# Third expert's rows gathered during the first expert's second product, and row traffic spread alike for all experts

## The chip, the cores and the metric

The kernel runs on one core of a Trainium2 chip. The metric is the time of one execution in device microseconds (us). Five engines work side by side, each with its own instruction queue in program order: PE (TensorE, matrix products), DVE (VectorE), ACT (ScalarE), POOL (GpSimd) and SP (SyncE, which here only issues transfers). Transfers (DMA) are issued by SP or POOL and then run on 16 DMA engines by themselves.

## The reference

Three stages follow one another: a decaying linear attention, a mixture of eight experts of which each row uses two, and a SoLU block. The middle stage is the one that the change touches:

```python
logits = x @ w_gate
noisy_logits = logits + np.log1p(np.exp(x @ w_noise)) * noise
top2 = np.argpartition(-noisy_logits, 2, axis=1)[:, :2]      # two experts for each of 1536 rows
...
for e in range(E):                                           # E = 8, D = 512, F = 1024
    for k in range(2):
        mask = top2[:, k] == e
        h = np.maximum(x[mask] @ w1[e], 0.0)                 # first product
        out[mask] += top2_w[mask, k, None] * (h @ w2[e])     # second product
```

All in float32.

## The kernel before

The experts are taken in an order by their number of rows, the first with room for 448 rows and the last for 384. The text calls them e0 to e7 in that order, so "the third expert" is e2. For each expert the program has a **first product** (`hidden`, L693: eight groups f = 0 to 7 of 12 matmuls, four by `xh` with two weights each and four by `xl`) and a **second product** (`second`, L1030: four steps j = 0 to 3 of 24 matmuls). A float32 product is made of three matmuls on a high and a low part: `split_unit` makes `wh` (ACT, L194) and `wl` (DVE, L195) from each raw weight tile `wr`; `xg_t` makes `xh` (ACT, L995) and `xl` (DVE, L996) from the rows of the next expert, in four pieces d = 0 to 3, during the second product of the expert before it.

How the rows of an expert reach `xg_t` is what the change is about. `load_xg(e)` is a generator whose steps are called from the main loop:

- up to four gathers on POOL (L959), each of 128 rows of `xd` (DRAM) into a buffer `xr` (on-chip);
- the stores of `xr` to `xs` in DRAM on SP (L969), two a step;
- the loads of `xq` from `xs` on SP (L976), two a step. These put the rows into 32x32 blocks, so that `xg_t` can turn them with a DVE transpose (`xt`, L993).

For e1 there is only the gather: PE transposes those rows itself (L989). For e2 and later all three steps are needed. In the kernel before, e2 gathers in the steps f = 0 to 3 of e1's first product, stores in f = 4 and 5 and loads in f = 6 and 7, while e3 gathers in f = 4 to 7 of the same product and stores and loads in j = 0 to 3 of e1's second product. All later experts do as e3 does, one expert earlier than they are needed. A one-element copy `pace` on POOL (L1060, L1068) ahead of a gather makes POOL wait for the result of group f. All experts share four `xr` buffers.

The order on each engine is the order in which the program issues. Around the change, SP's queue also has the weight loads (L176, `load_unit`; a load waits until the tile that it overwrites has been split), the stores of the finished rows (`yg`, L1017, in f = 5), and a conversion of the last block's weights that runs in pieces in between (`convert`: load `raw` L102, store `co` L125, work on DVE L117 to L124). `advance` splits the next weight units and issues loads for up to three units beyond. `weights()` (DVE, L661 to L679) runs once, in e1's second product.

Of the kernel before, what the change touches and what calls it, by code (L numbers as in the profile page):

```python
# [8 lines left out]
F32 = mybir.dt.float32  # L9
# [35 lines left out]
def retnet_moe_solu(ctx, tc, qT, kT, k, v, w_gate, w_noise, noise, w1, w2, w_in, w_out, g_ln,  # L45
                    decay, out, dbg=None):
    nc = tc.nc
# [4 lines left out]
    E = w1.shape[0]  # L52
    DM = H * D
# [39 lines left out]
    def convert_steps():  # L93
        V = nc.vector
        cv = conv_ctx.enter_context(tc.tile_pool(name="cv", bufs=1, side="right", reuse_waits="tile"))
        view = lambda x, c: x.rearrange("(p r) f -> p (r f)", p=128)[:, c:c + 512]

        def load(n):
            if n < len(conv_jobs):
                w, _, c = conv_jobs[n]  # L100
                t = cv.tile([128, 512], I64, tag="raw", name="raw", bufs=2)
                nc.sync.dma_start(t, view(w, c))  # L102
                raws.append(t)

        raws = []
        load(0)
        for n, (w, f, c) in enumerate(conv_jobs):
            load(n + 1)
            yield
            raw = raws.pop(0)  # L110
            bits = raw.bitcast(I32).rearrange("p (n t) -> p n t", t=2)
            l, h = raw.bitcast(U32).rearrange("p (n t) -> p n t", t=2)[:, :, 0], bits[:, :, 1]
            m, e = (cv.tile([128, 512], I32, tag=t, name=t) for t in ("cm", "ce"))
            t = cv.tile([128, 512], F32, tag="ct", name="ct")
            o = cv.tile([128, 512], F32, tag="co", name="co", bufs=2)

            V.tensor_scalar(m, h, 0xFFFFF, 1 << 20, op0=OP.bitwise_and, op1=OP.bitwise_or)  # L117
            V.scalar_tensor_tensor(t, l, 2.0 ** -32, m, op0=OP.mult, op1=OP.add)
            V.tensor_scalar(e, h, 0x7FF00000, None, op0=OP.bitwise_and)
            nc.scalar.activation(e, e, AF.Relu, bias=rebias, scale=8.0)  # L120
            yield

            V.scalar_tensor_tensor(e, h, -2 ** 31, e, op0=OP.bitwise_and, op1=OP.bitwise_or)
            V.scalar_tensor_tensor(o, t, 2.0 ** -20, e.bitcast(F32), op0=OP.mult, op1=OP.mult)  # L124
            nc.sync.dma_start(view(f, c), o)  # L125

    conv = convert_steps()

    def convert():
        next(conv, None)  # L130
# [87 lines left out]
    px = ex_ctx.enter_context(tc.tile_pool(name="px", bufs=1))  # L218
# [170 lines left out]
    for b in range(B):  # L389
        for r in range(2):  # L390
            t = wk.tile([128, HP, 128], F32, name=f"S{b}{r}", bufs=1)
# [180 lines left out]
    def add_table(lo):  # L572
        oh, nm = HOT.pop(lo)
        last = oh.shape[1] - 1
        p = bank("a", (128, 32))
        for n in range(last + 1):
            nc.tensor.matmul(p, oh[:, n], nm[:, n], start=(n == 0), stop=(n == last))
        nc.vector.tensor_add(table, table, p)  # L578
# [3 lines left out]
    def by_rows():  # L582

        m = [128, 4, 32]
        nc.vector.tensor_mul(spread, part4[:, :, None].to_broadcast(m), table[:, None, :].to_broadcast(m))
# [27 lines left out]
    def first_xt(part, d):  # L613

        n = BLKS[2 * part][1]
        p = bank("a", (128, 2, 2 * n)) if n <= 128 else None
        for s in range(2):
            for b in range(2):
                nc.tensor.transpose(p[:, s, b * n:(b + 1) * n], x0[2 * part + b][:n, (d + s) * 128:(d + s + 1) * 128],
                                    ident[:n, :n])  # L620
        hi, lo = xgT[0]
        at = BLKS[2 * part][0]
        nc.scalar.activation(hi[:, d:d + 2, at:at + 2 * n], p, AF.Copy)
        nc.vector.tensor_sub(lo[:, d:d + 2, at:at + 2 * n], p, hi[:, d:d + 2, at:at + 2 * n])
# [24 lines left out]
    pace = const.tile([1, 1], F32, name="pace")  # L649

    def lists():

        p = bank("a", (128, E - 1, 4))
        nc.tensor.matmul(p, spread.rearrange("p a i -> p (a i)"), sort.rearrange("p e s -> p (e s)"),
                         start=True, stop=True)
        nc.vector.tensor_scalar_min(rows_r, p, float(NT * 128 - 1))
# [27 lines left out]
    def hidden(e, f, c):  # L684

        xh, xl = xgT[e]
        hh, hl = H_t[e]
        early_part = not e and c.start == 0
        p = bank(("b", "c0", "b", "c1")[f % 4] if early_part else "ba"[f % 2])[:, :c.stop - c.start]

        terms = [(unit_t[8 * e + d][n], x, d) for x, ns in ((xh, (0, 1)), (xl, (0,))) for d in range(KD) for n in ns]
        for n, (w, x, d) in enumerate(terms):
            nc.tensor.matmul(p, w[:, 0, f * 128:(f + 1) * 128], x[:, d, c],  # L693
                             start=(n == 0), stop=(n == len(terms) - 1))
        nc.scalar.activation(hh[:, f, c], p, AF.Relu)  # L695
        nc.vector.scalar_tensor_tensor(hl[:, f, c], p, 0.0, hh[:, f, c], op0=OP.max, op1=OP.subtract)

    H_t = {}
# [5 lines left out]
    def hidden_of(e):  # L704
        H_t[e] = (ep.tile([128, KF, CAP], F32R, tag="hh", name="hh"),
                  ep.tile([128, KF, CAP], F32R, tag="hl", name="hl"))
# [241 lines left out]
    for p in range(2):  # L948
        first_xt(1, 2 * p)

    def load_xg(e):

        if e >= E:
            return

        n = SETS[e]
        t = [px.tile([128, DM], F32, tag="xr", name="xr", bufs=4) for b in range((n + 3) // 4)]
        for b in range(len(t)):
            nc.gpsimd.indirect_dma_start(  # L959
                out=t[b], out_offset=None, in_=xd[:],  # L960
                in_offset=bass.IndirectOffsetOnAxis(ap=rows_r[:, e - 1, b:b + 1], axis=0))
            yield
        if e == 1:
            xr_t[e] = t
            return
        xs = dram.tile([ROOM, DM], F32, tag="xs", name="xs", bufs=2)
        for b in range(len(t)):
            m = min(128, 32 * n - 128 * b)
            nc.sync.dma_start(xs[b * 128:b * 128 + m, :], t[b][:m])  # L969
            if b == 1:  # L970
                yield
        yield
        x = xr_t[e] = ep.tile([128, CAP // 32, 128], F32, tag="xq", name="xq", bufs=2)
        src = xs[:32 * n, :].rearrange("(b i) (a c) -> a i b c", i=32, a=4)
        for a in range(4):
            nc.sync.dma_start(x[32 * a:32 * a + 32, :n], src[a])  # L976
            if a == 1:
                yield
# [60 lines left out]
            convert()  # L1039
        feed(up, up + 3)  # L1040

    rows = None
    for e in range(E - 1):
        if e:
            hidden_of(e)
        for j in range(4):
            for f in (2 * j, 2 * j + 1):
                hidden(e, f, slice(0 if e else EARLY, CAPS[e]))
                if not e and f == 0:
                    add_table(4)  # L1050
                    add_table(10)
                    by_rows()
                if not e and f == 2:
                    lists()
                    for _ in load_xg(1):
                        pass
                    rt_ctx.close()
                if e == 1 and f < 4:
                    rows = rows or load_xg(2)
                    nc.gpsimd.tensor_copy(pace, H_t[e][0][:1, f, :1])  # L1060
                    next(rows)
                elif e and f > 3:
                    if e == 1:
                        next(rows, None)
                    if f == 4:
                        fresh = load_xg(e + 2)
                    if e + 2 < E:
                        nc.gpsimd.tensor_copy(pace, H_t[e][0][:1, f, :1])  # L1068
                        next(fresh)
                if f in (1, 3, 4, 5):  # L1070
                    d = (1, 3, 4, 5).index(f)
                    if e:
                        y_t(e - 1, d)
                    y_bank(e, d)
                elif e and f in (2, 6):
                    convert()
            advance(e, j)
        for j in range(4):
            unit_t.pop(8 * e + j)
        xgT.pop(e)  # L1080
        py = PY[e]
        for j in range(4):
            second(e, j, py)
            for d in ((0,), (1, 2), (3,), ())[j]:
                xg_t(e + 1, d)
            if e == 1 and j == 1:
                weights()
            advance(e, 4 + j)
            if e:
                next(fresh, None)  # L1090


    for _ in conv:
        pass
    e = E - 1
# [17 lines left out]

    w2_of = [unit_t.pop(8 * e + 4 + j) for j in range(4)]
    conv_ctx.close()
    m2_ctx = ExitStack()
    feed(n_units - 2, n_units)
    fr = m2_ctx.enter_context(tc.tile_pool(name="fr", bufs=2, side="right", reuse_waits="tile"))
# [204 lines left out]
```

## Time and profile before

| | |
|---|---|
| time, median of 3 runs | 557.49 us (556.52 to 558.67) |
| profiled execution | 557.17 us, of which the span of the trace is 555.4 us |
| PE busy | 523.2 us, 94% of the span |
| DVE, ACT, POOL busy | 367.1 us, 230.8 us, 100.8 us |
| mean granted TensorE clock | 0.959 of full speed |
| DMA | 111.92 MB, mean 202 GB/s |

The profiled execution lies 0.32 us under the median. "Busy" counts time in which an instruction runs; what matters for the end is where PE, the engine with most work, has to wait, and for whom.

### The profile page before, as it was taken

The numbers are of one execution on the slowest core, as the hardware profiler recorded it, in microseconds if no ns is written. First come the engines' busy times: TensorE is split into PE (matmuls) and PEld (weight loads), VectorE is DVE, ScalarE is ACT, GpSimd is POOL, SyncE is SP. The second block draws the span as 40 slices with busy tenths as digits, with TensorE's granted clock in tenths as the row PEclk, the third lists the DMA queues.
The fourth block names the chain that finished last, engine by engine and source line by source line (L and its number), as shares of the span: only waits on it lengthen the run. The fifth ranks groups of instructions, "written<-read, shape, count | busy, mean of one in ns | idle before, by whom it ended". The sixth has DMA issues, their size and how long they took to land.

```text
span 555.4 us, 8653 instructions
## 1 busy us (share of the span) xinstructions
PE 523.2 (94%) x3107; PEld 476.7 (86%) x3107; DVE 367.1 (66%) x718; ACT 230.8 (42%) x426; POOL 100.8 (18%) x202
## 2 busy tenths in 40 slices
PE   7999989799999279999999999999989999999996
PEld 6898968699998179999999999999868888888886
DVE  3577675657850788787787867887536677576650
ACT  2377712245520335344343433534544545444441
POOL 3000011040431004013030030000044463241110
PEclk9799987899999579999999999999999999999999
DMA  8898514256789289799799897885853456555431
GB/s 243 316 321 288 190 30 136 73 180 204 255 245 243 78 251 263 287 209 343 245 265 322 188 336 234 214 232 150 234 152 114 142 149 220 155 150 141 106 114 43
DMA packets 71857, 111.92 MB, mean 202 GB/s; under 512 B 9760, under 2 KB 37152, under 8 KB 71808
## 3 DMA queue, kind: packets, MB, share of 16 engines
q1 hardware_dynamic: 65520, 94.58, 58.1%
q0 software_dynamic: 4944, 16.39, 9.6%
q8 instruction: 26, 0.43, 0.3%
q10 hardware_dynamic: 1344, 0.34, 0.3%
q14 instruction: 23, 0.19, 0.1%
HBM read 83.50 MB, written 27.79 MB: 200 GB/s over the span
## 4 chain that ended last, share of the span: by engine, by line
PE 52%; DVE 15%; DMA 13%; issue 8%; ACT 6%; SPq 3%; POOL 2%; DVEq 0%; POOLq 0%; ACTq 0%
PE b L915 12%; PE d L828 12%; PE b L693 6%; PE c L1030 6%; PE a L693 6%; DVE wl L195 3%; DMA xq<-xs 3%; DMA wr<-in_moe_w_dram 2%; DVE xt L993 2%; DMA yg<-yr 2%; PE c L439 2%; PE c L473 2%; PE s L422 2%; DMA xr<-xd,rows_r 2%; ACT xh L995 1%
## 5 line engine op out<-in xcount | busy, mean ns | idle before, releaser
L195 DVE TENSOR_TENSOR wl<-wr,wh 128x1024 fp32r<-128x1024 f32 x68 | 81.6, 1220 | 21.6 <-ACT wh L194 20.9
L1030 PE MATMUL c<-hh,wh 128*128 128x448 f32 (+5 forms) x224 | 79.2, 354 | 0.3 <-DVE c L1004 0.3
L1030 PE MATMUL c<-hh,wl 128*128 128x448 f32 (+5 forms) x224 | 78.8, 352 | 0.0
L1030 PE MATMUL c<-hl,wh 128*128 128x448 f32 (+5 forms) x224 | 78.6, 351 | 0.0
L194 ACT ACTIVATE wh<-wr 128x1024 fp32r<-128x1024 f32 x68 | 69.8, 1050 | 9.1 <-DMA wr<-in_moe_w_dram 9.1
L693 PE MATMUL b<-xh,wh 128*128 128x192 f32 (+8 forms) x144 | 49.6, 351 | 15.2 <-ACT xh L995 14.9
L693 PE MATMUL b<-xh,wl 128*128 128x192 f32 (+8 forms) x144 | 48.2, 342 | 0.0
L693 PE MATMUL a<-xh,wh 128*128 128x256 f32 (+7 forms) x128 | 44.8, 353 | 0.6 <-DVE table L578 0.6
L693 PE MATMUL a<-xh,wl 128*128 128x256 f32 (+7 forms) x128 | 44.2, 349 | 0.0
L693 PEld LDWEIGHTS b<-xh,wh 128*128 128x128 f32 x144 | 28.4, 197 | 18.2 <-ACT xh L995 17.4
L995 ACT ACTIVATE xh<-xt 128x428 fp32r<-128x428 f32 (+5 forms) x24 | 12.9, 539 | 74.6 <-DVE xt L993 72.5
L1030 PEld LDWEIGHTS c<-hh,wh 128*128 128x128 f32 x224 | 42.1, 188 | 1.7 <-issue 0.6
L1030 PEld LDWEIGHTS c<-hl,wh 128*128 128x128 f32 x224 | 42.2, 188 | 1.1
L1030 PEld LDWEIGHTS c<-hh,wl 128*128 128x128 f32 x224 | 42.1, 188 | 1.2
L789 POOL DMA_INDIRECT y<-yg,slot_y x24 | 24.0, 1001 | 84.6 <-DMA yg<-y 73.7
L828 PE MATMUL d<-wh,x2h 128*128 128x512 f32 x96 | 38.7, 403 | 0.6 <-issue 0.6
L915 PE MATMUL b<-wh,zh 128*128 128x512 f32 (+1 forms) x104 | 38.4, 375 | 0.0
L915 PE MATMUL b<-wl,zh 128*128 128x512 f32 (+1 forms) x104 | 38.3, 375 | 0.0
L828 PE MATMUL d<-wh,x2l 128*128 128x512 f32 x96 | 37.7, 393 | 0.4 <-DVE x2l L813 0.4
L828 PE MATMUL d<-wl,x2h 128*128 128x512 f32 x96 | 37.4, 390 | 0.0
L1068 POOL COPY pace<-hh 1x1 f32<-1x1 f32 x20 | 10.7, 537 | 132.9 <-ACT hh L695 132.4
L993 DVE STREAM_TRANSPOSE xt<-xq 128x416 f32<-128x416 f32 (+2 forms) x24 | 21.9, 912 | 18.6 <-DMA xq<-xs 18.6
(235 smaller groups left out, 1092.7 us busy)
## 6 DMA issues: line engine op xcount, KB each, us to landing
wr<-in_moe_w_dram SPq DMA_DIRECT2D x60, 512.0 KB
zd<-zs SPq DMA_DIRECT2D x40, 128.0 KB
zc<-zd SPq DMA_DIRECT2D x10, 512.0 KB
xs<-xr SPq DMA_DIRECT2D x18, 256.0 KB
raw<-in_moe_w_in_dram SPq DMA_DIRECT2D x8, 512.0 KB
raw<-in_moe_w_out_dram SPq DMA_DIRECT2D x8, 512.0 KB
xq<-xs SPq DMA_DIRECT2D x16, 208.0 KB
yg<-yr SPq DMA_DIRECT2D x16, 208.0 KB
```

The lines of the kernel that those rows point to most:

```text
L194: nc.scalar.activation(hi, t, AF.Copy)
L195: low = lambda: nc.vector.tensor_sub(lo, t, hi)
L422: nc.tensor.matmul(p[:, s, hp, :], KT[i][r, hp, :], QT[i][r, hp, :], start=True, stop=True)
L439: nc.tensor.matmul(py[s * 64:s * 64 + 64, hp, :], VP[i][:, 2 * hp + s, :], PM[i][hp // 2][:, hp % 2, s, :], start=(not c), stop=True, skip ...
L473: nc.tensor.matmul(lg_all[:, i], XT[i][:, d, :], wgn[:, d, :], start=(d == 0), stop=(d == KD - 1))
L693: nc.tensor.matmul(p, w[:, 0, f * 128:(f + 1) * 128], x[:, d, c], start=(n == 0), stop=(n == len(terms) - 1))
L789: nc.gpsimd.indirect_dma_start(out=t, out_offset=None, in_=yg[:upto], in_offset=bass.IndirectOffsetOnAxis(ap=slot_y[:, i, s:s + 1], axis=0))
L828: nc.tensor.matmul(PH[i][:, s, :], x[:, c], w[:, 0, f], start=(n == 0), stop=(n == 3 * KD - 1))
L915: nc.tensor.matmul(p, z[:, f * 128:(f + 1) * 128], unit_t[8 * E + 4 + f // 2][n][:, f % 2, c], start=(m == 0), stop=(m == len(terms) - 1))
L993: nc.vector.transpose(t[:, :32 * n], xr_t[e][:, :n, d:128:KD])
L995: nc.scalar.activation(hi, t, AF.Copy)
L1030: nc.tensor.matmul(py[d][:, :CAPS[e]], c, h[:, f, :CAPS[e]], start=(f == 0 and n == 0), stop=(f == KF - 1 and n == 2))
```

## The change

A pool `gx` of four `xr` buffers is opened in e0's first product, once the routing stage's memory is free; e1's rows stay in the old buffers, those of e2 and later go to `gx`. The tile `ct` of the conversion goes away (its values overwrite `cm`), so the conversion's tiles take 2 KB less in each partition and `gx` takes 8 KB.

e2 now gathers in e0's second product (two gathers each in j = 0 and 1, without a `pace`), and stores in j = 2 and 3. For e3 and later the gathers stay in f = 4 to 7 two products ahead; the stores move from j = 0 and 1 to j = 1 and 2, and the loads from j = 2 and 3 to f = 1 and 3 of the next first product. e2's loads stand in f = 1 and 3 of e1's first product likewise.

```diff
-            t = cv.tile([128, 512], F32, tag="ct", name="ct")
+            t = m.bitcast(F32)
...
+    gx = {}
+    gx_ctx = ExitStack()
+
     def load_xg(e):
...
-        t = [px.tile([128, DM], F32, tag="xr", name="xr", bufs=4) for b in range((n + 3) // 4)]
+        t = [(px if e == 1 else gx["pool"]).tile([128, DM], F32, tag="xr", name="xr", bufs=4) for b in range((n + 3) // 4)]
...
-    rows = None
...
                     rt_ctx.close()
-                if e == 1 and f < 4:
-                    rows = rows or load_xg(2)
+                    gx["pool"] = gx_ctx.enter_context(tc.tile_pool(name="gx", bufs=1, side="right"))
+                if e and f in (1, 3):
+                    next(rows, None)
+                if e and e + 2 < E and f > 3:
+                    fresh = fresh if f > 4 else load_xg(e + 2)
                     nc.gpsimd.tensor_copy(pace, H_t[e][0][:1, f, :1])
-                    next(rows)
-                elif e and f > 3:
-                    if e == 1:
-                        next(rows, None)
-                    if f == 4:
-                        fresh = load_xg(e + 2)
-                    if e + 2 < E:
-                        nc.gpsimd.tensor_copy(pace, H_t[e][0][:1, f, :1])
-                        next(fresh)
+                    next(fresh)
...
             advance(e, 4 + j)
-            if e:
+            if not e:
+                fresh = fresh if j else load_xg(2)
+                for n in range(2 if j < 2 else 1):
+                    next(fresh)
+            elif j in (1, 2):
                 next(fresh, None)
+        rows = fresh
...
     conv_ctx.close()
+    gx_ctx.close()
```

On POOL, behind the loads of e1's first weights, the program had a `pace` ahead of each of e2's gathers. Of before:

```order
L176 DMA wr<-in_moe_w_dram 128x1024
L176 ISA
L176 DMA wr<-in_moe_w_dram 128x1024
L1060 CAST pace<-hh 1x1
L959 DMA xr<-xd,rows_r 128x512
L1060 CAST pace<-hh 1x1
L959 DMA xr<-xd,rows_r 128x512
```

Of the change, at the same place:

```order
L176 DMA wr<-in_moe_w_dram 128x1024
L176 ISA
L176 DMA wr<-in_moe_w_dram 128x1024
L962 DMA xr<-xd,rows_r 128x512 x4
L1065 CAST pace<-hh 1x1
L962 DMA xr<-xd,rows_r 128x512
```

The four gathers of e2 stand right behind the weight loads; the next `pace` is that of e3's first gather.

On SP, in e1's first product, e2's four stores stood behind e1's and e2's weight loads and ahead of e0's results, and its four loads behind these. Of before:

```order
L125 DMA w_in_70<-co 128x512
L102 DMA raw<-in_moe_w_in_dram 128x512
L176 ISA
L176 DMA wr<-in_moe_w_dram 128x1024
L969 DMA xs<-xr 128x512 x3
L969 DMA xs<-xr 64x512
L1017 DMA yg<-yr 32x14x128 x4
L176 ISA
L176 DMA wr<-in_moe_w_dram 128x2x512
L976 DMA xq<-xs 32x14x128 x4
```

Of the change, from the first weight load of e2 on:

```order
L176 DMA wr<-in_moe_w_dram 128x1024
L972 DMA xs<-xr 128x512 x3
L972 DMA xs<-xr 64x512
L979 DMA xq<-xs 32x14x128 x2
L176 ISA
L176 DMA wr<-in_moe_w_dram 128x1024
L176 ISA
L176 DMA wr<-in_moe_w_dram 128x1024
L125 DMA w_in_70<-co 128x512
L102 DMA raw<-in_moe_w_in_dram 128x512
L979 DMA xq<-xs 32x14x128 x2
```

Stores and first two loads moved ahead of two of e2's weight loads, and the last two loads ahead of e2's fourth weight load and of e0's results.

On SP, in e5's first product (the rows are those of e6, the weights too). Of before:

```order
L176 DMA wr<-in_moe_w_dram 128x1024
L976 DMA xq<-xs 32x13x128 x4
L176 ISA
L176 DMA wr<-in_moe_w_dram 128x1024
L176 ISA
L176 DMA wr<-in_moe_w_dram 128x1024
L125 DMA w_out_71<-co 128x512
L102 DMA raw<-in_moe_w_out_dram 128x512
```

Of the change:

```order
L972 DMA xs<-xr 32x512
L979 DMA xq<-xs 32x13x128 x2
L176 ISA
L176 DMA wr<-in_moe_w_dram 128x1024
L176 ISA
L176 DMA wr<-in_moe_w_dram 128x1024
L125 DMA w_out_71<-co 128x512
L102 DMA raw<-in_moe_w_out_dram 128x512
L979 DMA xq<-xs 32x13x128 x2
```

Two of the four loads moved behind two weight loads, a store of the conversion and its next load.

## Rows read from the trace of the kernel before

**Rows 1.** Busy time by stretch (us); last columns: granted clock, DMA share, GB/s.

```profile
130.00:140.00 10.00, 10.00 (x53) 9.27 (x52) 8.19 (x12) 5.21 (x8) 0.00 (x0) 1.00 0.79 250
...
178.90:203.50 24.60, 9.70 (x27) 7.22 (x27) 17.59 (x35) 7.38 (x11) 0.00 (x0) 0.58 0.52 148
...
240.00:400.00 160.00, 159.69 (x876) 157.73 (x876) 122.92 (x191) 70.56 (x105) 17.91 (x23) 1.00 0.89 249
```

**Rows 2.** Waits, whole span: us in total, times, longest.

```profile
DVE xt L993 <- DMA xq<-xs: 18.6, 1, 18.6
...
PE b L693 <- ACT xh L995: 14.9, 4, 7.3
```

**Rows 3.** Timeline of PE, end of e1's second product: start, duration, instruction.

```profile
178.72 0.36 PE L1030 MATMUL c<-hl,wh 128*128 128x448 f32 x1
178.92 0.37 PE L1030 MATMUL c<-hh,wl 128*128 128x448 f32 x1
182.13 0.73 PE L693 MATMUL b<-xh,wh 128*128 128x428 f32 x1 [2.85 <-ACT xh L995]
```

**Rows 4.** Chain of waits, 120 to 300 us: start, duration, what.

```profile
152.86 8.96 DMA xr<-xd,rows_r
...
169.88 10.45 DMA xq<-xs
180.46 0.98 DVE xt L993
...
196.82 0.57 ACT xh L995
197.43 2.51 PE b L693 x6
199.94 3.58 PE a L693 x12
203.51 2.36 PE b L693 x12
...
255.40 4.89 DMA wr<-in_moe_w_dram
```

**Rows 5.** Timeline of POOL.

```profile
122.34 0.54 POOL L176 DMA_DIRECT2D wr<-in_moe_w_dram  x1 [2.47 <-DVE wl L195]
...
146.59 1.02 POOL L959 DMA_INDIRECT xr<-xd,rows_r  x1 [0.53 <-ACT hh L695]
...
164.33 0.97 POOL L959 DMA_INDIRECT xr<-xd,rows_r  x1 [9.42 <-DMA xs<-xr]
```

**Rows 6.** Tile xr: time from issue to landing of its gathers.

```profile
DMA to landing us min/median/max: 5.6/7.9/9.0
```

**Rows 7.** Timeline of SP.

```profile
144.05 0.34 SPq L176 DMA_DIRECT2D wr<-in_moe_w_dram  x1
...
144.63 0.34 SPq L176 DMA_DIRECT2D wr<-in_moe_w_dram  x1
...
196.68 0.87 SPq L969 DMA_DIRECT2D xs<-xr  x2
...
202.77 0.85 SPq L976 DMA_DIRECT2D xq<-xs  x2
...
318.68 0.43 SPq L102 DMA_DIRECT2D raw<-in_moe_w_out_dram  x1
```

**Rows 8.** Timelines of ACT and DVE, end of e1's first product.

```profile
155.44 1.05 ACT L194 ACTIVATE wh<-wr 128x1024 fp32r<-128x1024 f32 x1
...
161.25 0.62 DVE L696 SCALAR_TENSOR_TENSOR hl<-a,hh 128x448 fp32r<-128x448 f32 x1 [1.22 <-ACT hh L695]
```

**Rows 9.** Timelines of DVE, ACT and PE, from e5's second product to e6's first.

```profile
330.16 0.91 DVE L993 STREAM_TRANSPOSE xt<-xq 128x416 f32<-128x416 f32 x1
...
342.34 0.53 ACT L995 ACTIVATE xh<-xt 128x388 fp32r<-128x388 f32 x1 [2.97 <-DVE xt L993]
...
342.92 0.45 PE L693 MATMUL b<-xh,wh 128*128 128x388 f32 x1
```

## The prediction

> **What bounds the kernel now.** I read the busy time by stretch first [rows 1]. From 240 to 400 us, nearly five experts long, PE is busy for 159.69 of 160 us at the full granted clock: there the matmuls are the bound, and no transfer is worth anything. The stretch from 178.9 to 203.5 us is different: PE is busy for 9.70 of 24.60 us, the granted clock falls to 0.58 (so much of it ran at 1.2 GHz instead of 2.4), and the DMA share is only 0.52. Next the waits [rows 2]: PE waited 14.9 us in four waits for `xh`, and DVE once 18.6 us for `xq`. PE's timeline places it [rows 3]: the last matmul of e1's second product starts at 178.92, and the first of e2's first product at 182.13. Last the chain of waits [rows 4], which says why: e2's last gather is issued at 152.86 and lands 8.96 us later, stores and loads follow, the last `xq` load has been issued by 169.88 and lands 10.45 us later, and only at 180.46 can DVE begin `xt`. The fourth piece of `xh` ends at 196.82 + 0.57 = 197.39. The cause stands on POOL [rows 5]: its last weight load ends at 122.88, and the first gather of e2 runs only at 146.59, after the result of e1's first group.
>
> **What the stall costs.** Matmuls of this kind start 178.92 - 178.72 = 0.20 us apart [rows 3], so unbroken work would have begun e2 at 179.12. A group of 12 takes 2.36 us at full clock [rows 4]; two groups would end at 183.84. They ended at 199.94 + 3.58 = 203.52 [rows 4]. So 19.7 us is the most that this place can give. In it, the last 6 and the next 12 matmuls took 2.51 + 3.58 = 6.09 us where 18 at full clock take 3.54: 2.55 us of the 19.7 is the slow clock after the wait.
>
> **The change, part by part.**
>
> *Gathers of e2.* Four `pace` copies go, and the four gathers run from 122.88, some 1.3 us apart (164.33 and its successors are of that kind [rows 5]), so to about 128. At the slowest landing of a gather, 9.0 us [rows 6], all are there by 137. I cost them nothing: PE works on e0's second product, and the DMA share in 130 to 140 is 0.79 [rows 1], so there is some room for 1 MB. Without that room they would hold e1's later weights back by 1 MB at 250 GB/s [rows 1], 4 us.
>
> *Stores and loads of e2.* On SP the stores stand behind e2's first weight load, which was issued at 144.05 [rows 7]; that does not move, so they start at 144.4. Two stores take 0.87 us [rows 7], four end at 146.2. The first two loads must wait until the stores have landed: for e3 that was from 196.68 + 0.87 = 197.55 to 202.77, 5.2 us [rows 7]. So SP stands until 151.4: **this is a new wait**, with two of e2's weight loads behind it. The two loads take 0.85 us [rows 7], the two weight loads some 0.9, the conversion's store and load 0.9, and the second two loads end at about 155.1. For their landing I have 5.6 us, the fastest gather [rows 6], to 10.45 us, `xq` itself beside e3's gathers [rows 4]: 160.7 to 165.5. These gathers no longer wait 9.4 us for `xs` [rows 5] and start near 155, so the same company remains, and I take 8 us: 163.1.
>
> The Trainium skill's page "DMA: Bandwidth & Descriptors", section "Anatomy of one DMA — SWDGE (gpsimd) path", fits a transfer alone at about 2.0 us plus its bytes over 436 GB/s. By it the two loads (448 KB) would take an estimated 3.1 us and land at 158.2; no wait of DVE for them would be left, and the sum below would come out at an estimated 538.3 us. By the row of 10.45 us, three times as long for these transfers in company, it would be 539.8; the measurement decides which is nearer.
>
> *What waits behind SP.* The second of e2's weight loads was issued at 144.63 [rows 7] and would now go out near 152.7. A weight load landed 4.89 us after its issue elsewhere [rows 4]: 157.6. ACT split that tile at 155.44 [rows 8], so ACT and then DVE come 2.2 us later. DVE's last work for e1's first product ended at 161.25 + 0.62 = 161.87 [rows 8]; now about 164.0. From there DVE turns e2's rows. In the old trace that took from 180.46 to 197.39, 16.9 us (four transposes and splits, three weight splits, `weights()`, a conversion), with all data there, and I see nothing that shortens it. So `xh` is complete at 164.0 + 16.9 = 180.9. PE needs the fourth piece at the seventh matmul of e2, 179.12 + 6 x 0.20 = 180.3. Residue: 0.6 us. At the lower ends it is nothing (161.87 + 16.9 = 178.8, 1.5 us early), at the upper 165.5 + 16.9 - 180.3 = 2.1 us, with the slow clock 4.7. I take 1.0.
>
> *Stores and loads of e3 to e7.* Moving the stores by one step costs nothing while PE has 16 to 18 us of second product to cover them. The loads lose more. Closest is e6: in the new order its last two loads follow the conversion's load, issued at 318.68 [rows 7], and end near 320.1. DVE wants them at 330.16 [rows 9]: 10.0 us for landing. The fourth `xh` of e6 ends at 342.34 + 0.53 = 342.87 and PE takes it at 342.92 [rows 9], so there is no slack behind it. Read in the same way, the other four (the pattern repeats, slack to PE's need included) leave 11.7 us for e4, 12.4 for e5, 14.6 for e3 and 15.4 for e7. With 5.6 to 10.45 us for a landing only e6 can lose, 0 to 0.4 us; I take 0.2.
>
> *`ct`.* DVE's instructions keep number, shape and place; one overwrites its input. Nothing. The conversion's tiles lie elsewhere, but its first work is done in e0's second product, when the routing stage's memory is long free.
>
> *Sum*, against the profiled execution: 557.2 - 19.7 + 1.0 + 0.2 = 538.7 us. The median of the runs lies 0.3 us above that execution: **539.0 us**.
>
> **Rivals.**
>
> *Late at e2 only.* If the new wait on SP and the traffic of 144 to 165 us stretch the landing of e2's loads to 15 us (170.1), the residue is 170.1 - 164.0 + 0.6 = 6.7 us, plus 2.55 us of slow clock: 557.2 - 19.7 + 9.3 + 0.3 = 547.1 us. For it: the traffic is moved together with weight loads and e3's gathers. Against it: no landing in the rows is longer than 10.45 us. 0.20 for 541.5 to 552, and 0.03 for 552 to 554.7.
>
> *Slower: loads late at every expert.* The mechanism is the loads of f = 1 and 3, which land a fixed time L after SP issues them. e2 tolerates about 8.0 us (180.3 - 16.9 - 155.1 = 8.3, less for the weights), e6 10.0, the others as above. At L = 14 the stalls are 6.0 + 4.0 + 2.3 + 1.6 = 13.9 us, and with 2.55 us of slow clock at each of the four 24.1 us: 557.2 - 19.7 + 24.1 + 0.3 = 561.9 us. It decides from L near 13, where stalls and clock (9.9 + 10.2) eat the gain. Against it: that is 2.5 us beyond the longest landing seen, and that one was beside a DMA queue with gathers, weights and results in it. 0.06.
>
> *The change doesn't do what it says.* If the gathers still ran no earlier than 146.59, because their buffers or their list were not ready, nothing would move: 557.5 us. But the list feeds e1's gathers, which run before 122.88, and `gx` takes memory of the routing stage, which has ended. 0.05 for 554.7 to 560.3.
>
> *More than the stall.* A smoother DMA stream could also shave waits elsewhere; with PE at 159.69 of 160 [rows 1] there is next to nothing to shave. 0.04 for less than 536.
>
> **How the numbers follow.** The forecast, 536 to 541.5 us, has 0.62. The range of 536 to 548 takes it and most of the first rival, 0.62 + 0.17 = 0.79; its lower end is the sum without any residue (537.8) less what PE's few other waits could give, its upper end the residue of the first rival. A measurement of this kernel can tell some 0.5% (2.8 us) from no change. Faster by more: 0.62 + 0.20 + 0.03 + 0.04 = 0.89. Within: 0.05. Slower: 0.06. The forecast's own range is 537 to 541.5, from residues of 0 to 3.5 us.
>
> **What would show it.** Right: gathers of e2 on POOL from 123 us without a wait, stores on SP at about 144.4, first `xq` loads some 5 us after them, DVE's first `xt` of e2 between 162 and 166 us, PE's wait for `xh` at 179 us under 3 us or gone, the granted clock at 1.00 from 160 to 240 us, and e6's start shifted by the same amount as e3's. Wrong: stores of e2 not before 150 us; a wait of DVE for `xq` of over 3 us at any expert; a PE wait at the start of e3 to e7; or ACT waiting for weights in e1's first product for more than 3 us, since everything on DVE then comes later by as much.

## The result, and the profile after

| | before | after | ratio, 95% interval |
|---|---|---|---|
| median of 20 runs each | 558.17 us (556.52 to 560.84) | 550.34 us (544.93 to 557.27) | 0.9843 [0.982, 0.9867] |
| the change run again (`e1_after_again`) | 557.95 us | 551.97 us (549.12 to 553.31) | 0.9867 [0.9813, 0.9921] |

The change is faster by 1.6%, and by 1.3% when run again: 6 to 9 us. I had forecast 539.0 us, 18 us faster, with a range up to 548: the direction was right, the size less than half, and the result lies outside the range. The profiled execution of the first group (555.16 us) is one of the two slow ones of its 20 runs, so the rows here are from the change run again (553.31 us, span 551.6 us). Lines of the program behind the new pool stand three lower: the gathers are L962, the stores L972, the loads L979, `xt` L996, `xh` L998.

The windows cut the time after at the starts of products: e2's first and second product, then the first products of e5 and e6. The columns are the length, the busy time of each engine, the granted clock, the DMA share and its GB/s:

```profile
core 0: us, PE busy (x) PEld busy (x) DVE busy (x) ACT busy (x) POOL busy (x), PEclk, DMA share, GB/s
181.12:206.48 25.36, 20.39 (x97) 19.34 (x96) 21.08 (x42) 9.99 (x15) 3.82 (x5) 0.93 0.83 226
206.48:225.04 18.56, 18.56 (x97) 18.05 (x96) 13.87 (x20) 7.25 (x10) 3.18 (x4) 1.00 0.85 301
296.54:317.84 21.30, 19.11 (x98) 18.77 (x97) 16.56 (x28) 8.47 (x13) 3.05 (x4) 0.92 0.64 187
335.12:355.38 20.26, 17.28 (x97) 16.86 (x97) 16.46 (x28) 9.88 (x16) 0.00 (x0) 1.00 0.76 235
```

A product that PE runs without a pause has the length of its busy time at full clock. e2's second product does (18.56 of 18.56 us). e2's first product, with the same 96 matmuls, takes 25.36 us: 6.8 us are lost there, 4.97 of them in one wait and the rest at a granted clock of 0.93. Before, this product took 35.34 us after a start that was 3.0 us late. So most of the old stall is gone, but not all, and two new losses stand at e5 and e6, where PE had none before [rows 1]. The one wait in e2's first product:

```profile
182.08 0.36 PE L693 MATMUL b<-xh,wl 128*128 128x428 f32 x1
187.42 0.46 PE L693 MATMUL b<-xh,wh 128*128 128x428 f32 x1 [4.97 <-ACT xh L998]
```

The waits from 130 to 420 us (in all, times, longest) say the same; the rows before are PE's 14.9 us and DVE's 18.6 us [rows 2]:

```profile
ACT wh L194 <- DMA wr<-in_moe_w_dram: 14.2, 5, 4.3
PE b L693 <- ACT xh L998: 10.4, 4, 5.0
DVE xt L996 <- DMA yg<-yr: 4.4, 2, 2.5
DVE xt L996 <- DMA xq<-xs: 2.2, 1, 2.2
```

PE's four waits for `xh` were all at e2 before; now they are 4.97 us at e2, 2.19 at e5, 2.98 at e6 and a short one. DVE waits for rows three times, 6.6 us in all, where it waited once for 18.6 us. (That two of the three are put down to the results `yg` is a matter of which transfer's event came last; `xt` needs `xq`, and at e2 the last load of `xq`, issued at 158.77, landed 11.6 us later, at 170.4.) ACT waits 14.2 us for weights, against 9.1 us in the kernel before.

Now the start of e2, engine by engine. POOL issues e2's gathers right behind the weight loads; before, they stood at 146.59 and later [rows 5]:

```profile
124.08 0.54 POOL L176 DMA_DIRECT2D wr<-in_moe_w_dram  x1 [2.30 <-DVE wl L195]
124.93 1.02 POOL L962 DMA_INDIRECT xr<-xd,rows_r  x1 [0.30 <-issue]
...
128.79 1.12 POOL L962 DMA_INDIRECT xr<-xd,rows_r  x1 [0.30 <-issue]
```

SP in e1's first product shows, in each line, the start, the duration and the number of issues in a row:

```profile
146.15 0.34 SPq L176 DMA_DIRECT2D wr<-in_moe_w_dram  x1
146.61 2.43 SPq L972 DMA_DIRECT2D xs<-xr  x4
153.93 0.85 SPq L979 DMA_DIRECT2D xq<-xs  x2
155.03 0.97 SPq L176 DMA_DIRECT2D wr<-in_moe_w_dram  x2
156.04 0.43 SPq L125 DMA_DIRECT2D w_in<-co  x1
156.51 0.43 SPq L102 DMA_DIRECT2D raw<-in_moe_w_in_dram  x1
156.99 2.54 SPq L979 DMA_DIRECT2D xq<-xs  x2
```

Between the end of the stores at 149.04 and the first loads at 153.93 SP does nothing: it stands until the stores have landed (the last was issued at 148.01 and landed 5.87 us later, at 153.88), and two weight loads stand behind it. ACT and DVE then take those weights and rows:

```profile
161.83 1.06 ACT L194 ACTIVATE wh<-wr 128x1024 fp32r<-128x1024 f32 x1 [4.29 <-DMA wr<-in_moe_w_dram]
```

```profile
170.41 0.97 DVE L996 STREAM_TRANSPOSE xt<-xq 128x448 f32<-128x448 f32 x1 [2.48 <-DMA yg<-yr]
```

and the chain of waits ends in PE's seventh matmul of e2, which runs at 187.42 where 182.08 + 0.19 = 182.27 was its turn:

```profile
185.89 0.89 DVE xt L996
186.80 0.57 ACT xh L998
187.42 2.25 PE b L693 x6
```

The same pattern shows in e5's first product, in which e6's rows are loaded. SP:

```profile
303.79 0.34 SPq L176 DMA_DIRECT2D wr<-in_moe_w_dram  x1
304.23 0.85 SPq L972 DMA_DIRECT2D xs<-xr  x2
310.21 0.84 SPq L979 DMA_DIRECT2D xq<-xs  x2
311.24 0.98 SPq L176 DMA_DIRECT2D wr<-in_moe_w_dram  x2
...
313.21 2.83 SPq L979 DMA_DIRECT2D xq<-xs  x2
```

ACT, DVE and PE behind it:

```profile
318.41 1.06 ACT L194 ACTIVATE wh<-wr 128x1024 fp32r<-128x1024 f32 x1 [4.19 <-DMA wr<-in_moe_w_dram]
```

```profile
326.57 0.92 DVE L996 STREAM_TRANSPOSE xt<-xq 128x416 f32<-128x416 f32 x1 [2.22 <-DMA xq<-xs]
```

```profile
339.32 0.45 PE L693 MATMUL b<-xh,wh 128*128 128x388 f32 x1 [2.98 <-ACT xh L998]
```

SP stands from 305.08 to 310.21, ACT waits 4.19 us for a weight, DVE 2.22 us for rows, and PE 2.98 us at the start of e6. In e3's first product, ahead of e4, SP stands in the same way from 229.18 to 234.14, but there PE loses only 0.5 us.

The largest of the new losses, at e5, doesn't have this pattern. SP in e4's first product, in which e5's rows are loaded:

```profile
264.50 0.96 SPq L972 DMA_DIRECT2D xs<-xr  x2
268.72 0.33 SPq L125 DMA_DIRECT2D w_out<-co  x1
269.10 1.12 SPq L102 DMA_DIRECT2D raw<-in_moe_w_out_dram  x1
271.19 0.84 SPq L979 DMA_DIRECT2D xq<-xs  x2
272.22 0.98 SPq L176 DMA_DIRECT2D wr<-in_moe_w_dram  x2
```

```profile
280.44 1.06 ACT L194 ACTIVATE wh<-wr 128x1024 fp32r<-128x1024 f32 x1 [3.00 <-DMA wr<-in_moe_w_dram]
```

```profile
299.99 0.45 PE L693 MATMUL b<-xh,wh 128*128 128x396 f32 x1 [2.19 <-ACT xh L998]
```

A store and a load of the conversion stand between the stores and the loads, and SP waits only 0.97 us for the landing (270.22 to 271.19). The loads and the two weights behind them are late all the same, since the stores are: the first loads go out 10.3 us after the start of e4's first product, and ACT waits 3.00 us for one of the weights.

### The profile page after: what moved, and what is told of

Its sections match the earlier page's. It is cut to its first block, busy times and chain, and to the rows that moved or that the text cites. A ratio compares the mean times of both kernels' runs of the same rounds, so it can differ in the third digit from the quotient of the medians.

```text
span 553.4 us, 8650 instructions
## 1 busy us (share of the span) xinstructions
PE 523.1 (95%) x3107; PEld 477.9 (86%) x3107; DVE 367.2 (66%) x718; ACT 230.4 (42%) x426; POOL 99.0 (18%) x198
## 2 busy tenths in 40 slices
DMA packets 71857, 111.92 MB, mean 202 GB/s; under 512 B 9760, under 2 KB 37152, under 8 KB 71808
## 4 chain that ended last, share of the span: by engine, by line
PE 55%; DMA 16%; DVE 15%; ACT 5%; issue 5%; SPq 3%; POOL 0%; DVEq 0%; ACTq 0%; POOLq 0%
PE b L915 12%; PE d L828 12%; PE c L1033 7%; PE b L693 7%; PE a L693 6%; DMA xq<-xs 6%; DVE wl L195 3%; DMA vt<-in_v_dram 3%; DVE xt L996 2%; DMA wr<-in_moe_w_dram 2%; DMA xs<-xr 2%; ACT xh L998 2%; PE c L473 2%; PE c L439 2%; DVE xl L999 1%
## 5 line engine op out<-in xcount | busy, mean ns | idle before, releaser
L693 PE MATMUL b<-xh,wh 128*128 128x192 f32 (+8 forms) x144 | 49.2, 348 | 11.1 <-ACT xh L998 10.8
L1065 POOL COPY pace<-hh 1x1 f32<-1x1 f32 x20 | 12.5, 623 | 156.7 <-ACT hh L695 156.7
L998 ACT ACTIVATE xh<-xt 128x428 fp32r<-128x428 f32 (+5 forms) x24 | 13.0, 540 | 65.7 <-DVE xt L996 65.7
L693 PE MATMUL b<-xl,wh 128*128 128x192 f32 (+8 forms) x144 | 32.4, 348 | 2.0 <-DVE xl L624 1.9
```

Source lines behind the costliest of these rows:

```text
L998: nc.scalar.activation(hi, t, AF.Copy)
```

## The experiments

Three theories were set against each other. **A, the stand:** what is missing is lost because SP stands some 5 us for the landing of stores, directly ahead of the rows' loads, and holds weight loads behind it; it happens at e2 and, since the stores were moved by one step, at e4 and e6 too. **B, the transfers:** the DMA engines are full from 145 to 172 us, and something comes late whatever the order. **C, the place of the loads:** f = 1 and 3 are simply too late for rows that DVE wants at the start of the second product. All kernels below are the change with one edit, unless said otherwise. They ran in three groups, and each is compared with the runs of the kernel before in its own group.

| kernel | median, us | before, us | ratio, 95% interval |
|---|---|---|---|
| `e1_after_again` | 551.97 | 557.95 | 0.9867 [0.9813, 0.9921] |
| `e2_only` | 544.98 | 557.95 | 0.9747 [0.9696, 0.9797] |
| `e2_sooner` | 541.26 | 557.95 | 0.9697 [0.964, 0.9755] |
| `spread_only` | 563.12 | 557.95 | 1.0091 [1.0046, 1.0136] |
| `stores_back` | 545.60 | 557.95 | 0.9747 [0.9682, 0.9812] |
| `e2_stores_sooner` | 545.19 | 557.95 | 0.9765 [0.9727, 0.9803] |
| `e3_gathers_late` | 549.00 | 557.95 | 0.9857 [0.981, 0.9903] |
| `weights_first` | 543.47 | 557.95 | 0.9752 [0.9714, 0.9791] |
| `all_stores_sooner` | 538.45 | 559.06 | 0.9643 [0.9595, 0.9691] |
| `all_sooner_weights_first` | 538.42 | 559.06 | 0.9648 [0.9599, 0.9696] |
| `weights_first_again` | 542.23 | 559.06 | 0.9701 [0.9652, 0.975] |
| `e2_sooner_again` | 539.68 | 559.06 | 0.9649 [0.9598, 0.9701] |

**The change again**, without an edit.

> The changed kernel itself, for a second profile and a paired time. Theory A (the order on SP): e2's stores start only behind e2's first weight load, SP then stands some 5 to 8 us for their landing, and the last xq load of e2 is issued near 159 us and lands 10 us or more later; PE waits at the start of e2 for 5 to 9 us and for 1 to 4 us in all at the starts of e4 and e6. Time near 550 us, ratio 0.98. Theory B (the transfers themselves): the same waits, since DMA is full from 145 to 172 us whatever the order; the same time. This run alone does not tell them apart.

It stands at 551.97 us, 1.6 us over the first median, with the rows shown above.

**e2 alone as changed**, e3 and later as before:

```diff
-                if e and f in (1, 3):
+                if e == 1 and f in (1, 3):
                     next(rows, None)
...
-            elif j in (1, 2):
+            else:
                 next(fresh, None)
```

> Only e2's gathers, stores and loads are moved as in the changed kernel; from e3 on stores and loads stand where they stood before (j = 0 to 3 of the second product). Theory A: the wait at e2 stays at 5 to 9 us, the waits at e4 and e6 go, so 2 to 5 us less than the changed kernel, about 546 us. If the spread of the later experts costs nothing: the same as the changed kernel, 550 us.

544.98 us, 7.0 us less than the change. So the spreading for e3 and later, which I had priced at 0.2 us, costs about 7. The windows of e2's, e5's and e6's first products:

```profile
181.94:207.46 25.52, 20.28 (x97) 19.27 (x96) 21.19 (x42) 10.06 (x16) 3.72 (x5) 0.93 0.76 222
297.06:314.34 17.28, 17.28 (x98) 17.28 (x97) 14.50 (x27) 8.17 (x13) 3.13 (x5) 1.00 0.93 231
331.62:348.58 16.96, 16.96 (x98) 16.96 (x97) 13.71 (x26) 8.97 (x14) 0.00 (x0) 1.00 0.88 235
```

e2 loses as much as in the change, and e5 and e6 nothing.

**The spreading alone**, in the kernel before:

```diff
+                if e > 1 and f in (1, 3):
+                    next(late, None)
...
-            if e:
+            if e and j in (1, 2):
                 next(fresh, None)
+        if e:
+            late = fresh
```

> The other half alone: e2 as before the change (paced gathers in e1's first product), but stores of e3 and later in j = 1 and 2 and loads in f = 1 and 3 of the next first product. Theory A: the big wait at e2 stays, and 1 to 5 us are lost at e4 and e6: 559 to 563 us, ratio 1.00 to 1.01. If the spread costs nothing or helps: 558 us or less.

563.12 us, 5.2 us slower than the kernel before: this part of the change does harm by itself, without anything that e2 does.

**e2 alone, and sooner**: gathers in j = 0, stores in j = 1 and loads in j = 2 of e0's second product, e3 and later as before:

```diff
-                if e and f in (1, 3):
-                    next(rows, None)
...
-                for n in range(2 if j < 2 else 1):
-                    next(fresh)
-            elif j in (1, 2):
+                for n in range((4, 2, 2, 0)[j]):
+                    next(fresh, None)
+            else:
                 next(fresh, None)
-        rows = fresh
```

> e2's four gathers in j = 0 of e0's second product, its stores in j = 1, its loads in j = 2, so that all stand ahead of or right behind e2's first weight load on SP; later experts as before the change. Theory A: xq of e2 is on chip by about 155 us, DVE starts its transposes at 162 to 164 us, PE waits under 2 us at e2: 538 to 542 us. Theory B: DMA is as full as it was, other transfers come late in place of xq (weights of e2 or the rows of e3), PE still waits 4 us or more at e2 or e3: 545 to 550 us.

541.26 us, and 539.68 us when it was run again (below). B had asked for 545 to 550 us: with the same 111.92 MB moved in another order the loss at e2 goes (18.63 us for e2's first product), so the amount moved isn't what costs the time there. In the change, the DMA share is also well under one while SP stands, at e2 and in e5's first product:

```profile
149.04:153.93 4.89, 4.89 (x26) 4.53 (x25) 4.86 (x8) 3.14 (x5) 0.00 (x0) 1.00 0.67 251
305.08:310.21 5.13, 5.13 (x30) 5.13 (x29) 4.55 (x8) 3.95 (x8) 0.00 (x0) 1.00 0.56 192
```

**Stores of e3 and later back** to j = 0 and 1, the loads left in f = 1 and 3:

```diff
-            elif j in (1, 2):
+            elif j < 2:
                 next(fresh, None)
```

> The changed kernel, but from e3 on the stores stand in j = 0 and 1 again as before the change (the loads stay in f = 1 and 3, e2 stays as changed). Theory A (SP stands at the first loads until the second pair of stores has landed, and holds the weights behind them): with the stores earlier SP no longer stands there, the waits at e4 and e6 go, time as with e2 alone moved, 544 to 547 us. Theory C (the loads in f = 1 and 3 are simply too late): the waits at e4 and e6 stay, 549 to 552 us.

545.60 us. That is the time of `e2_only`, though the loads stand in f = 1 and 3. Its profile has e5's and e6's first products at their unbroken 17.27 and 16.96 us. So it is the stores' step that costs the 6 to 7 us and not the place of the loads: theory C falls for e3 and later.

**Stores of e2 sooner**, all in j = 1 of e0's second product, with its four gathers all in j = 0; e3 and later as in the change:

```diff
-                for n in range(2 if j < 2 else 1):
+                for n in range((4, 2, 0, 0)[j]):
                     next(fresh)
```

> The changed kernel, but e2's four gathers stand in j = 0 of e0's second product and its four stores in j = 1, ahead of e2's first weight load on SP; its loads stay in f = 1 and 3 of e1. Theory A: SP does not stand at e2's first loads, ACT does not wait for the weights, xq of e2 is there by 162 us, PE waits under 2 us at e2; the waits at e4 and e6 stay: 543 to 546 us. Theory C: loads in f = 1 and 3 land 12 us after their issue as now, the wait at e2 shrinks by no more than the 5 us by which they are issued sooner, to 2 to 4 us: 546 to 549 us.

545.19 us, some 6 us less than the change: the other half. In its profile (of a run of 552.87 us, the longest of the five) e2's first product has its unbroken length (186.19 to 204.75, 18.56 us).

**Gathers of e3 late**, all four in f = 7 of e1's first product, out of the company of e2's loads:

```diff
-                if e and e + 2 < E and f > 3:
+                if e and e + 2 < E and f > (6 if e == 1 else 3):
...
-                    next(fresh)
+                    for _ in range(4 if e == 1 else 1):
+                        next(fresh)
```

> The changed kernel, but e3's four gathers all wait for f = 7 of e1's first product in place of f = 4 to 7, so that e2's loads have no gathers beside them. If the company of the gathers is what makes e2's xq land 12 us after its issue: it lands 3 us or more sooner and the wait at e2 shrinks by 2 to 4 us, 547 to 549 us. If not (the loads lie behind weights and a conversion load on SP's own queue, and are slow by themselves): 550 to 552 us.

549.00 us, at the edge of the two ranges expected; its interval and that of the change overlap almost wholly. The trace says more: with no gather beside them, e2's second pair of loads landed 10.8 and 11.6 us after issue, where the change has 11.6 and 12.3. So the company of the gathers is worth some 0.8 us of the landing, and not what is missing.

**Weights first**: the first loads of the rows in f = 2, behind the two weight loads:

```diff
-                if e and f in (1, 3):
+                if e and f in (2, 3):
                     next(rows, None)
```

> The changed kernel, but the first two loads stand in f = 2 in place of f = 1, behind the two weight loads on SP that they held up; the second two stay in f = 3. Theory A, its part on the weights: ACT's wait of 3.5 to 4.3 us for weights in the first products of e1, e3 and e5 goes, but xq is no sooner; the waits of PE shrink by what the weights made of them, 1 to 3 us in all: 547 to 550 us. If the weights make nothing of the waits (xq alone decides): 550 to 552 us.

543.47 us, and 542.23 us when run again: less than either range expected. SP at e2:

```profile
144.85 2.60 SPq L972 DMA_DIRECT2D xs<-xr  x4
147.70 1.68 SPq L176 DMA_DIRECT2D wr<-in_moe_w_dram  x2
152.06 0.86 SPq L979 DMA_DIRECT2D xq<-xs  x2
...
153.96 1.32 SPq L979 DMA_DIRECT2D xq<-xs  x2
```

SP still stands, from 149.38 to 152.06, but the weights have gone out before it. The waits from 130 to 420 us:

```profile
DVE xt L996 <- DMA xq<-xs: 3.4, 2, 2.6
PE b L693 <- ACT xh L998: 1.1, 1, 1.1
ACT wh L194 <- DMA wr<-in_moe_w_dram: 0.9, 2, 0.5
```

ACT's 14.2 us for weights are gone and 8 to 9 us of time with them. But ACT's waits for weights don't measure the loss by themselves: in `e2_sooner_again` they are 11.4 us, and PE waits 0.2 us. And this edit doesn't isolate the weights quite: the second loads of e2 also end 2.5 us sooner than in the change, counted from the start of e1's first product (155.28 - 140.43 = 14.85 us against 159.53 - 142.21 = 17.32).

**All stores one step sooner**, for e2 (its gathers again all in j = 0) and for e3 and later, with the loads in f = 1 and 3:

```diff
-                for n in range(2 if j < 2 else 1):
+                for n in range((4, 2, 0, 0)[j]):
                     next(fresh)
-            elif j in (1, 2):
+            elif j < 2:
                 next(fresh, None)
```

> The change with the stores one step sooner at every expert: e2 gathers four times in j = 0 and stores in j = 1 of e0's second product, e3 and later store in j = 0 and 1; the loads stay in f = 1 and 3. Theory A (the cost is SP standing some 5 us for the landing of the second pair of stores, with weight loads behind it): the stand is gone everywhere, ACT's waits for weights between 130 and 420 us fall from 14 us to under 6, and the time is 539 to 544 us, below that of the kernel with sooner stores at e3 and later alone (545.6). Theory C (loads that land too late in f = 1 and 3 as such): DVE still waits for rows at e2 and e6, and the time stays at 545 to 549 us.

538.45 us, 12 to 14 us less than the change and under the 539.0 us that I had forecast for the change. SP in e1's first product, and the windows of the first products of e2, e5 and e6:

```profile
143.79 0.34 SPq L176 DMA_DIRECT2D wr<-in_moe_w_dram  x1
145.89 0.85 SPq L979 DMA_DIRECT2D xq<-xs  x2
146.97 1.78 SPq L176 DMA_DIRECT2D wr<-in_moe_w_dram  x2
```

```profile
178.69:197.25 18.56, 18.56 (x97) 18.05 (x96) 15.22 (x28) 9.32 (x14) 3.59 (x5) 1.00 0.94 231
286.85:304.13 17.28, 17.28 (x97) 17.28 (x97) 15.70 (x28) 8.14 (x13) 4.43 (x6) 1.00 0.91 233
321.41:338.37 16.96, 16.96 (x98) 16.96 (x97) 13.67 (x26) 9.20 (x14) 0.00 (x0) 1.00 0.76 223
```

No stores stand ahead of the loads, SP doesn't stand for 5 us, and PE runs all three products without a pause. The loads are in f = 1 and 3 as in the change, so theory C falls for e2 as well.

**All stores sooner and weights first**, both edits:

> The same, and the first loads of the rows go to f = 2, behind the two weight loads. Theory A: with no stand on SP left to avoid, putting the weights first is worth nothing more: within 2 us of the kernel with all stores sooner, 539 to 544 us. If the two were independent costs (the stand, and the rows' loads taking the queue ahead of the weights), it would be faster again by 2 to 5 us: 535 to 540 us.

538.42 us, the same. Once the stand is gone, the order of weights and rows on SP is worth nothing that these runs can tell: they were one cost, not two.

**The two repetitions** in the same group of runs:

> The change with the first loads in f = 2 behind the two weight loads, run again beside the two others: 541 to 545 us, ACT's waits for weights under 2 us.

> The kernel before with e2 alone moved, and that to gathers, stores and loads in j = 0, 1 and 2 of e0's second product, run again beside the others: 540 to 543 us. It is the version to beat; theory A expects the kernel with all stores sooner within 2 us of it, since neither has a stand on SP at e3 and later.

542.23 and 539.68 us. `all_stores_sooner` and `e2_sooner` are equal within their spread (535.95 to 539.82 and 536.79 to 542.51 us); both beat the kernel before and the change.

## Why the prediction was right in direction and wrong in size

**Right.** The stall at e2 was there to be had: 19.7 us by the rows, and `all_stores_sooner`, which has no pause left at e2, e5 and e6, gains 20.6 us. The gathers run behind the weight loads without a wait, from 124.93 us. The stores, the stand and DVE's chain came as worked out. Counted from the start of e1's first product, which is 2.00 us later than before (142.21 against 140.21), they compare so:

| step at e2, in the time of the kernel before | predicted | measured |
|---|---|---|
| stores start on SP | 144.4 | 144.61 |
| stand ends, first loads go out | 151.4 | 151.93 |
| second loads issued | 155.1 | 157.53 |
| their landing | 8 us | 10.88 us |
| rows there for DVE | 163.1 | 168.41 |
| ACT late for the weights behind SP | 2.2 us | 4.39 us |
| DVE free | 164.0 | 165.93 |
| from DVE's start to the fourth `xh` | 16.9 us | 16.96 us |
| residue, with slow clock | 1.0 us | 6.8 us |

**The step that failed** is the one on e3 to e7: "Moving the stores by one step costs nothing while PE has 16 to 18 us of second product to cover them." I asked only whether the loads in f = 1 and 3 would be in time for DVE, and the answer to that was right: with the loads in f = 1 and 3 and the stores not ahead of them, nothing is lost. But the step brought the second pair of stores directly ahead of the first loads on SP in e3's and e5's first products, and there SP stands 5 us with two weight loads behind it, exactly the wait that I had named at e2 and had not looked for elsewhere. So e6's last loads were issued by 19.5 us after the start of e5's first product (316.04 - 296.54) where I had worked out 13.0 (320.1 - 307.1). DVE had no slack at e6 (the last `xh` ended 0.05 us before PE took it [rows 9]): ACT's 4.19 us for a weight and then DVE's 2.22 us for rows end in PE's 2.98. In the product lengths this term is 21.30 - 17.28 + 20.26 - 16.96 = 7.3 us, and 0.5 us at e4; `e2_only` gives 7.0 us, `spread_only` 5.2 us. From the start of e1's second product to the start of e7 the profiles give 211.2 us for the change against 203.1 for `e2_only`, and 223.9 for `spread_only` against 216.8 before: 8.1 and 7.1 us. That the stores' step costs this is shown by `stores_back`; by which path it costs 4.0 us at e5, where SP waits 0.97 us for the landing, is not shown. I had 0.2.

**The term that was mis-sized** is the residue at e2: 6.8 us for 1.0. The mechanism was the one described (SP stands, weights and rows come late, DVE's chain has no room), but the rows arrived 5.3 us later than taken: 2.9 us from the landing, 10.88 us and so past my upper end of 10.45, and the rest mostly from the second loads, whose issue took 2.54 us instead of 0.85. (I had added the 10.45 us to the end of an issue, but it is counted from the start of one; counted like that, this landing took 11.6 us.) PE's wait then brought the slow clock with it, at 1.8 us. With both terms as measured, 557.2 - 19.7 + 6.8 + 7.3 + 0.5 + 0.3 = 552.4 us, against 551.97 us for the change run again; the 20 runs of the first group have 550.34.

Of the rivals, "late at e2 only" (547.1 us) had the right mechanism for half of the loss, at a landing shorter than the 15 us which it asked for; "loads late at every expert" named the right places but the wrong cause, since the same loads cost nothing without the stores ahead of them. Of the four signs that I had listed as wrong, three came: PE's waits at e5 and e6, ACT's wait of over 3 us for weights, and DVE's wait for `xq`, though this only in the profile of the first group (3.6 us; 2.5 at most in the change run again). The stores of e2 were not late.

By the Trainium skill's page "DMA: Bandwidth & Descriptors", section "Anatomy of one DMA — SWDGE (gpsimd) path", the two loads would have landed after an estimated 3.1 us. That section's fit is for transfers issued by POOL (GpSimd), and these were issued by SP. The trace agrees only with its fastest loads of rows (3.0 us); their median is 7.7 us and the slowest took 12.6 us.

What stays open: how much of the stand's cost goes through the weights and how much through the rows, since every edit that freed the one also moved the other by some us. The trace gives an estimate only for the last part: DVE's waits for rows, which ended last, are 2.48 of PE's 4.97 us at e2 and 2.22 of 2.98 at e6.

## What to carry to other kernels

A store to DRAM and a load of the same data, one after the other on an in-order issuing queue, was here a wait of 4.9 to 5.3 us for everything queued behind, among it weight loads that the next engine waited for. Put other issues, or a whole step, between them, and when a schedule is made alike for all rounds, read the new order of the queue at each round: a wait that is named at one place can stand at the others. And price a landing by the slowest row of its kind plus the company that the change itself adds.

## What was not expected of the hardware

The loads of rows landed in 3.0 to 12.6 us, median 7.7, at 208 to 224 KB each (the change run again, 150 to 330 us). What was issued just ahead goes with it: at e2 the first pair, issued as the stand ended, landed 3.3 and 4.0 us after issue, and the second pair, 3 us later and behind two weight loads and a store and a load of the conversion (1.8 MB), 11.6 and 12.3 us. At e6 it was 3.3 and 3.9 us, then 11.3 and 12.6.

The time of a run varies more ahead of e1 than behind it: e1's first product began between 139.74 and 147.28 us in the profiles of these kernels, while from the start of e1's second product to the start of e7 `all_stores_sooner` took 196.1 us and `e2_sooner_again` 196.8 us, with spans of 534.3 and 540.8 us. What delays the start was not looked into; for a change in the experts from e1 on, that stretch is the better measure.
